# Layer 1 of the last chunk as a Strassen product, interleaved with layer 2 of the chunk ahead of it

## The chip, the cores and the metric

The kernel runs on one core of one Trainium2 chip. A core has five engines that matter here, each with its own in-order list of instructions: TensorE (PE, matmuls; its weight loads are shown apart as PEld), VectorE (DVE), ScalarE (ACT), GpSimd (POOL) and SyncE (SP, which here only starts DMAs). They meet through semaphores. TensorE writes to PSUM, eight banks of 512 fp32 columns; the other data are in SBUF. The metric is the device time of one execution in microseconds (us).

## The reference

The kernel computes attention and then a two-layer perceptron on its output.

- Attention: q, k, v are [8 batches, 8 heads, 576 tokens, 64]. Heads 0 to 3 see the last 32 positions, heads 4 to 7 see every 32nd earlier position; softmax, then the product with v.
- The heads are put side by side: x is [4608 tokens, 512].
- Layer 1: h = x @ w_in with w_in [512, 2048], then g = max(h, 0) + alpha * min(h, 0), with one alpha for each of the 2048 columns.
- Layer 2: out = g @ w_out with w_out [2048, 512], fp32.

## The kernel before, in words

Everything is written out by hand: each instruction goes through `keep`, which holds the program's order, so each engine executes its instructions in the order in which the Python code emits them. There is no scheduler that moves them.

The 4608 tokens are nine chunks of 512 (`NCH`, n = 0 to 8). Attention writes x transposed into a ring `xT`. For each chunk the main loop has 30 steps i. In steps 0 to 15 `lin1_piece` (L694 and after) makes one piece m of layer 1: 128 of the 2048 columns for 512 tokens, by four matmuls of 512 columns (`lin1_mm`, L678) into one of three PSUM banks `hb` that are used in turn. ScalarE then makes neg = Relu(-h) into one of three buffers in turn (L697), and VectorE makes g = neg * (1 - alpha) + h as fp16 into `gT` (L700). That last operation is not emitted at once: it is put in a list `late` and emitted a little later, when the next attention step or the end of the step empties the list.

In steps 16 to 29 `lin2_sums` makes layer 2 of the same chunk as a Strassen product in Winograd's form (for chunks 1 to 8). Tokens and the 2048 inner columns are cut in halves, and so is the output: seven products p0 to p6 stand for the eight quarter products. Each product has two row blocks (mt) of eight matmuls of 256 columns (L811), one row block for each step. The products need sums of quarters of g (`g_sum`, L760; the array `gsum`, called g1 to g4 here) and of quarters of w_out, which are made once. Three banks A, B and C collect the products: A takes p0, then p2, p4 and p6 on top of it, and between them it is copied out or added (L823 on ScalarE after p0, p1, p2 and p6; L826 on VectorE after p3, p4, p5). A bank may be written again only when the reader before has finished. Most of g1 is made by GpSimd during layer 1 (steps 5, 9 and 13); the rest of g1 and g2, g4, g3 are made by VectorE, emitted in the first steps of layer 2.

Between these steps `attn_n` emits pieces of attention for later batches. They run out during layer 2 of chunk 6: the last masks of the scores (L470, L477) are GpSimd's last work there. Chunks 7 and 8 have no attention beside them.

In chunk 8, layer 2 uses a further bank (`opl`) so that its results go out by halves.

Of the kernel before, what the change touches and what calls it, by code (L numbers as in the profile page):

```python
# [9 lines left out]
F32 = mybir.dt.float32  # L10
F16 = mybir.dt.float16
ALU = mybir.AluOpType
AF = mybir.ActivationFunctionType
# [19 lines left out]
def kernel(  # L33
# [36 lines left out]
    id16 = cpool.tile([16, 16], F32)  # L70
    alpha_r = cpool.tile([16, 128], F32)
    oma = cpool.tile([128, 16], F32)
    mmul = cpool.tile([128, 360], F16)
    madd = consts[:, 128:488]
    ident = consts[:, 0:128]
# [18 lines left out]
    NE = 6  # L94
# [2 lines left out]
    LX = 5  # L97
    qTs = [cpool.tile([128, 2, 672], F16, name=f"qT{i}") for i in range(2)]
    kTs = [cpool.tile([128, 2, (768, 672)[i]], F16, name=f"kT{i}") for i in range(2)]
    vls = [cpool.tile([128, 24, 65], F16, name=f"vl{i}") for i in range(2)]  # L100
    vss = [cpool.tile([128, 4, 8, 65], F16, name=f"vs{i}") for i in range(2)]
    ets = [cpool.tile([128, 800], F16, name=f"et{i}") for i in range(NE)]
    x16s = cpool.tile([80, 1024], F16)
    qks = {nm: cpool.tile([80, 4, 512], F16, name=f"{nm}sd") for nm in "qk"}

# [318 lines left out]
    late = []  # L424
# [152 lines left out]
    for g in range(7, npair + 2):  # L577
        c = g // 4
        a, p, t = g, g - 1, g + 1
# [69 lines left out]
    def attn_until(b):  # L649

        return max(i for i, (g, _) in enumerate(pieces) if g == 4 * b + 3) + 1

    def attn_step(end):
        run_masks()
        if pos["i"] < end:
            pieces[pos["i"]][1]()
            pos["i"] += 1
        while late:
            late.pop(0)()
        if defer:  # L660
            defer.pop(0)()


    gTs = {}
# [23 lines left out]
    def lin1_piece(n, m):  # L688
        if n not in gTs:
            gTs[n] = gpool.tile([128, 16, 512], F16, tag="gT", name="gT")  # L690
        if n == 0 and m < 3:
            hps = lin1_mm(n, m, (0,), False, True)
        else:
            hps = lin1_mm(n, m, (2, 3, 0, 1) if n == 1 else range(4), True, True)  # L694

        neg = npool.tile([128, 512], F32, tag="neg", name="neg")
        keep(nc.scalar.activation(neg, hps, AF.Relu, scale=-1.0))  # L697

        def fin():
            keep(nc.vector.scalar_tensor_tensor(  # L700
                gTs[n][:, m, :], neg, oma[:, m : m + 1], hps, op0=ALU.mult, op1=ALU.add))
        late.append(fin)
# [33 lines left out]
    def w_sums(eng, which):  # L736

        w1, w2, w4 = wsum
        w3 = wq(0, 1)
        steps = {  # L740
            1: (w1, wq(0, 1), wq(0, 0), ALU.subtract),
            2: (w2, wq(1, 1), w1, ALU.subtract),
            3: (w3, wq(1, 1), wq(0, 1), ALU.subtract),
            4: (w4, wq(1, 0), w2, ALU.subtract),
        }
        for z in which:
            o, x, y, op = steps[z]
            keep(eng.tensor_tensor(o, x, y, op=op))
# [26 lines left out]
    def lin2_sums(n, i):  # L775
# [69 lines left out]
        else:  # L845
# [7 lines left out]
            elif mt:  # L853
                store(n, 1, 0, o21)

    def load_w(c, second, half=None):
# [23 lines left out]
    def load_unit(b, strided, v_too=True):  # L880
# [3 lines left out]
        if v_too:  # L884
# [7 lines left out]
            name=nc.get_next_instruction_name(), act_func_set_id=6, ins=[], outs=[]  # L892
# [120 lines left out]
    load_unit(3, False, False)  # L1013


    for n in range(1, NCH):
        ab = attn_until(n + 1) if n + 1 < B else len(pieces)
        left = ab - pos["i"]
        acc = 0.0
        if n == 1:  # L1020
            w_sums(nc.vector, (3,))
        for i in range(30):
            second["on"] = i >= 16
            if i < 16:
                lin1_piece(n, {13: 7, 14: 14}.get(i, 8 * (i % 2) + i // 2))
                if i in (5, 9, 13) and (n, i) != (1, 13):
                    g_sum(nc.gpsimd, n, 1, i // 2 - 2, i // 2)
                if n == 1 and i == 14:
                    load_v(3, False)
            else:  # L1030
                lin2_sums(n, i - 16)
                if n == 1 and i == 20:
                    load_v(3, True)
            if n < B - 2 or i < 16 or i > 19:
                if n != 1 or i not in (16, 17):
                    acc += left / ((22.5 if i < 16 else 16.9) if n == 1 else 16 if n == B - 2 else 20.5) * (
                        0.5 if i < 16 else 1.0)
            cnt = int(acc)
            acc -= cnt
            attn_n(cnt, ab)  # L1040
        while pos["i"] < ab:
            attn_step(ab)


# [28 lines left out]
```

The softmax here doesn't subtract the row's maximum and nothing guards it: scores larger than these inputs give would overflow.

## Time and profile before

The median of three executions is 298.58 us (297.83 to 298.62). The profiled execution has a span of 296.6 us.

| Stretch of the span, us | what TensorE does | VectorE busy, us | ScalarE busy, us | GpSimd busy, us |
|---|---|---|---|---|
| 227.6 to 241.0 | layer 2 of chunk 6, the last of attention | 10.88 | 3.94 | 1.44 |
| 241.0 to 254.8 | layer 1 of chunk 7 | 10.58 | 9.64 | 3.47 |
| 254.8 to 267.0 | layer 2 of chunk 7 | 7.43 | 2.36 | 0 |
| 267.0 to 280.8 | layer 1 of chunk 8 | 10.54 | 9.54 | 3.47 |
| 280.8 to 296.6 | layer 2 of chunk 8, last outputs | 8.06 | 3.05 | 0 |

In the first four stretches TensorE is busy from end to end; in the last it is busy for 12.34 of 15.80 us, the rest being the last copy and the last DMA. The granted clock of TensorE is 1.00 in the first four.

A row of a group of instructions reads: line, engine, operation, what it writes <- what it reads, shape, count | busy time in us, mean ns of one | idle time of the engine ahead of it, and what ended that. In a row of the order of time the first number is the start in us from the start of the span, the second the length of the row.

### The profile page before, as it was taken

What the parts mean: (1) busy time and instruction counts of PE and PEld (TensorE: products, weight loads), DVE (VectorE), ACT (ScalarE), POOL (GpSimd) and SP (SyncE); (2) the same over time, 40 slices, a digit from 0 to 9 for tenths busy, and PEclk for the clock granted to TensorE, in tenths of its full rate; (3) what the DMA queues carried; (4) which work ended last, traced back from release to release, by engine and by line L of the source; (5) the groups of instructions that cost most, each with busy time, mean ns of one, the idle gap of its engine ahead of it and who ended that gap; (6) DMA issues with size and microseconds to landing.
All of it is one profiled execution on the core that took longest, in us unless ns stands there. A gap on an engine that the chain in (4) does not pass through costs nothing.

```text
span 296.6 us, 7099 instructions
## 1 busy us (share of the span) xinstructions
PE 289.7 (98%) x2808; PEld 193.9 (65%) x2808; DVE 227.8 (77%) x427; ACT 173.7 (59%) x325; POOL 168.0 (57%) x174
## 2 busy tenths in 40 slices
PE   7899999999999999999999999999999999999995
PEld 3564456645885487647898887468746864784584
DVE  6788869979966987588848884889488858936872
ACT  3566558889557763775367637763676157406620
POOL 8972269379738996688767777765564003101300
PEclk9999999999999999999999999999999999999999
DMA  7999999996998989999999999993811140022004
GB/s 217 208 200 207 205 239 262 180 198 233 119 139 146 167 89 159 175 151 165 147 222 146 147 132 194 202 127 64 192 22 21 25 141 0 2 74 71 0 2 141
DMA packets 102529, 41.01 MB, mean 138 GB/s; under 512 B 80720, under 2 KB 99424, under 8 KB 102496
## 3 DMA queue, kind: packets, MB, share of 16 engines
q0 software_dynamic: 56048, 18.20, 60.3%
q1 hardware_dynamic: 46176, 21.83, 38.1%
q10 hardware_dynamic: 272, 0.52, 0.6%
q8 instruction: 22, 0.36, 0.6%
q14 instruction: 11, 0.09, 0.1%
HBM read 38.60 MB, written 9.44 MB: 162 GB/s over the span
## 4 chain that ended last, share of the span: by engine, by line
PE 89%; DVE 4%; DMA 2%; ACT 2%; issue 1%; SPq 0%; ACTq 0%
PE hb L678 38%; PE hb L811 30%; PE hb L715 5%; PE pv L512 4%; DMA kl<-in_k_dram 2%; PE sp L450 2%; PE hx L678 2%; PE tp L280 2%; PE xp L533 1%; DVE gT L700 1%; PE opl L811 1%; PE sph L450 1%; DVE gsum L760 1%; PE pv L508 1%; ACT neg L697 1%
## 5 line engine op out<-in xcount | busy, mean ns | idle before, releaser
L678 PE MATMUL hb<-xT,win 128*128 128x512 f16 (+1 forms) x616 | 127.2, 357 | 0.0
L700 DVE SCALAR_TENSOR_TENSOR gT<-neg,oma,hb 128x512 f16<-128x512 f32 x138 | 100.6, 744 | 33.0 <-ACT neg L697 26.3
L697 ACT ACTIVATE neg<-hb 128x512 f32<-128x512 f32 x138 | 82.1, 598 | 32.7 <-PE hb L678 31.5
L678 PEld LDWEIGHTS <-win 128*128 128x128 f16 x640 | 59.9, 98 | 53.8
L760 POOL TENSOR_TENSOR gsum<-gT 128x512 f16<-128x512 f16 x23 | 26.5, 1150 | 68.8 <-DVE gT L700 68.8
L811 PEld LDWEIGHTS <-gsum 128*128 128x128 f16 x512 | 47.5, 98 | 5.9 <-DVE gsum L760 0.2
L811 PEld LDWEIGHTS <-gT 128*128 128x128 f16 x384 | 35.9, 98 | 6.0 <-issue 0.5
L470 POOL TENSOR_TENSOR et<-et,mmul 128x576 f16<-128x576 f16 (+1 forms) x24 | 30.5, 1273 | 12.9 <-issue 6.5
L823 ACT COPY o<-hb 128x512 f32<-128x512 f32 (+1 forms) x32 | 18.1, 569 | 32.5 <-PE hb L811 32.5
L523 DVE TENSOR_TENSOR x<-pv,rc 96x384 f16<-96x384 f32 (+2 forms) x65 | 34.5, 531 | 2.2
L811 PE MATMUL hb<-wout,gT 128*128 128x256 f16 x248 | 30.8, 273 | 0.1
L811 PE MATMUL hb<-wout,gsum 128*128 128x256 f16 x248 | 30.5, 272 | 0.2 <-ACT o L823 0.2
L811 PE MATMUL hb<-wsum,gsum 128*128 128x256 f16 x248 | 30.1, 273 | 0.0
L477 POOL TENSOR_TENSOR et<-et,mmul 72x576 f16<-72x576 f16 (+2 forms) x24 | 29.4, 1227 | 0.4 <-ACT et L474 0.4
L826 DVE TENSOR_TENSOR o<-hb,o 128x512 f32<-128x512 f32 (+1 forms) x24 | 16.3, 680 | 17.0 <-PE hb L811 12.5
L464 ACT ACTIVATE et<-sp 72x576 f16<-72x576 f32 (+2 forms) x24 | 16.4, 685 | 20.6 <-PE sph L450 17.2
L512 PEld LDWEIGHTS <-et 72*128 72x128 f16 (+1 forms) x416 | 21.8, 98 | 8.1 <-issue 1.3
L474 ACT ACTIVATE et<-sph 72x288 f16<-72x288 f32 (+2 forms) x48 | 17.8, 388 | 0.0
L521 DVE RECIPROCAL rc<-pv 72x6 f32<-72x6 f32 (+2 forms) x80 | 14.5, 181 | 2.7 <-PE pv L512 2.4
L715 PE MATMUL hb<-wout,gT 128*128 128x512 f16 x64 | 15.6, 379 | 0.3 <-ACT osb L720 0.3
L811 PE MATMUL hb<-wsum,gT 128*128 128x256 f16 x120 | 15.3, 273 | 0.0
L217 POOL COPY vs<-stv 72x1024 f16<-72x1024 f16 x12 | 12.1, 1031 | 4.0 <-DMA stv<-in_v_dram 4.0
(116 smaller groups left out, 320.2 us busy)
## 6 DMA issues: line engine op xcount, KB each, us to landing
out_dram<-o SPq DMA_DIRECT2D x31, 256.0 KB, 3.4
stv<-in_v_dram POOLq DMA_DIRECT2D x8, 288.0 KB, 8.4
vl<-in_v_dram POOLq DMA_DIRECT2D x6, 384.0 KB, 9.2
kl<-in_k_dram SPq DMA_DIRECT2D x4, 512.0 KB, 5.4
wout<-in_moe_w_out_dram POOLq DMA_DIRECT2D x4, 512.0 KB, 16.2
qsd<-in_q_dram POOLq DMA_DIRECT2D x6, 288.0 KB, 7.7
ksd<-in_k_dram POOLq DMA_DIRECT2D x6, 288.0 KB, 8.1
win<-in_moe_w_in_dram POOLq DMA_DIRECT2D x3, 512.0 KB, 12.2
```

The costliest lines, as they stand in the source:

```text
L470: keep(nc.gpsimd.tensor_tensor(mv, mv, m, op=ALU.mult))
L474: keep(nc.scalar.activation(ev[:, n * y : n * y + n], sps[y][0:r, 0:n], AF.Exp, scale=SCALE))
L477: keep(nc.gpsimd.tensor_tensor(mv, mv, m, op=ALU.mult))
L512: keep(nc.tensor.matmul(pv[:, 65 * x : 65 * x + 65], et[0:r, c : c + 128], v16[0:r, 2 * P.pr + hh, t, :] if P.strided else v16[:, 6 * (2 * ...
L523: keep(nc.vector.tensor_tensor(P.x16[0:w, c0 : c0 + 64 * nb].rearrange("r (c e) -> r c e", e=64), pvv[:, :, 0:64], rc[0:w, 0:nb].unsqueeze ...
L678: keep(nc.tensor.matmul(hps[:, dst : dst + w], win16[:, kk, 128 * m : 128 * m + 128], xT[:, kk, src : src + w], start=(first and kk == kks ...
L697: keep(nc.scalar.activation(neg, hps, AF.Relu, scale=-1.0))
L700: keep(nc.vector.scalar_tensor_tensor(gTs[n][:, m, :], neg, oma[:, m : m + 1], hps, op0=ALU.mult, op1=ALU.add))
L715: keep(nc.tensor.matmul(ops, gTs[n][:, kf, 128 * mt : 128 * mt + 128], wout16[:, kf, :], start=(kf == 0), stop=(kf == 15)))
L760: keep(eng.tensor_tensor(o[:, k0:k1], x[:, k0:k1], y[:, k0:k1], op=op))
L811: keep(nc.tensor.matmul(dst, lhs[:, kf, 128 * mt : 128 * mt + 128], rhs[:, kf, :], start=(first and own and kf == 0), stop=(kf == 7), skip ...
L823: keep(nc.scalar.copy(o, x))
```

## The change

Layer 1 of chunk 8 (called `NL`) is made by the same kind of product. The 512 input columns, the 512 tokens and the 2048 output columns are cut in halves; the output columns are further cut into four units v = 0 to 3, so that one unit has 256 columns of each half. A unit has seven products p0 to p6 of four matmuls of 256 columns each (`lin1_sums`). It needs four sums of quarters of w_in (`unit_sum`, on GpSimd) and, shared by all units, four sums of quarters of x (`x_sum`, on VectorE).

These products are no longer a stretch of their own: each step of layer 2 of chunk 7 is followed by two of them, so 14 steps hold all 28. Their results are collected in bank A (two banks in turn, for even and odd units), B and C. ScalarE copies A, B, A out after p0, p1 and p2; VectorE adds B, A, C onto these copies after p3, p4 and p5; p6 is finished from the bank itself. The activation then follows for each finished quarter [128, 2 x 256]: ScalarE's Relu and two half-width operations on VectorE, or, for p3 of every unit and p5 of units 1 and 3, four operations on GpSimd (twice min and times -(1 - alpha), with the scalar `noma`, then a sum). These last operations are deferred by `late` to just ahead of the next product.

The new g, `gT2`, would need SBUF of its own while chunk 7's is still in use; it takes the place of the attention buffers `vls`, `vss` and the sixth `ets`, which become views of it. The sums take buffers that attention used in the pools for q, k, x and v.

```diff
+    gT2 = cpool.tile([128, 16, 512], F16, name="gT2")
+    gflat = gT2.rearrange("p k c -> p (k c)")
+    vls = [gflat[:, 1560 * i : 1560 * i + 1560].rearrange("p (b e) -> p b e", e=65) for i in range(2)]
...
+    ets = [cpool.tile([128, 800], F16, name=f"et{i}") for i in range(NE - 1)] + [gflat[:, 7280:8080]]
...
+        bank, lhs, rhs, first = (
+            ("A", wh(v, 0, 0), xh(0, 0), True),
+            ("B", g1, xsums[0], True),
+            ("A", g2, xsums[1], False),
+            ("B", g4, xh(1, 1), False),
+            ("A", g3, xsums[2], False),
+            ("C", wh(v, 0, 1), xh(1, 0), True),
+            ("A", wh(v, 1, 1), xsums[3], False),
+        )[p]
+        t = hid[bank][v % 2]
+        for mm in range(2):
+            for kk in range(2):
+                keep(nc.tensor.matmul(
+                    t[:, 256 * mm : 256 * mm + 256], lhs[:, kk, 128 * mm : 128 * mm + 128], rhs[:, kk, :],
+                    start=(first and mm == 0 and kk == 0), stop=(kk == 1), skip_group_check=True))
+        tv = t.rearrange("p (m c) -> p m c", m=2)
+        if p < 3:
+            keep(nc.scalar.copy(hid[("o11", "o22", "o12")[p]], tv))
+            return
+        i, l = ((0, 1), (1, 1), (0, 0), (1, 0))[p - 3]
+        if p < 6:
+            o = hid[("o12", "o22", "o11")[p - 3]]
+            keep(nc.vector.tensor_tensor(o, o, tv, op=ALU.add))
+        else:
+            o = tv
+        neg = npool.tile([128, 2, 256], F32, tag="neg", name="neg")
+        pool = p == 3 or (p == 5 and v % 2 == 1)
+        if not pool:
+            keep(nc.scalar.activation(neg, o, AF.Relu, scale=-1.0))
+
+        def fin(o=o):
+            for mm in range(2):
+                m = 8 * i + 2 * v + mm
+                g = gT2[:, m, 256 * l : 256 * l + 256]
+                if pool:
+                    keep(nc.gpsimd.tensor_scalar(
+                        neg[:, mm], o[:, mm], 0.0, noma[:, m : m + 1], op0=ALU.min, op1=ALU.mult))
+                    keep(nc.gpsimd.tensor_tensor(g, neg[:, mm], o[:, mm], op=ALU.add))
+                else:
+                    keep(nc.vector.scalar_tensor_tensor(
+                        g, neg[:, mm], oma[:, m : m + 1], o[:, mm], op0=ALU.mult, op1=ALU.add))
+
+        late.append(fin)
...
+            if n == NL and i < 16:
+                continue
...
+            if n == NL - 2 and i >= 26:
+                unit_sum(nc.gpsimd, 0, i - 26)
+            if n == NL - 1:
+                if i < 16 and i % 2:
+                    unit_sum(nc.gpsimd, 1 + i // 8, i % 8 // 2)
+                if i == 4:
+                    keep(nc.vector.tensor_scalar(noma, oma, -1.0, None, op0=ALU.mult))
+                if i in (6, 8, 10, 12):
+                    x_sum(nc.vector, i // 2 - 3)
+                if 20 <= i < 24:
+                    unit_sum(nc.gpsimd, 3, i - 20)
+                if i >= 16:
+                    for v, p in slots[2 * (i - 16) : 2 * (i - 16) + 2]:
+                        while late:
+                            late.pop(0)()
+                        lin1_sums(v, p)
+                        if p == 1 and 0 < v:
+                            g_sum(nc.gpsimd, NL, 1, 2 * v - 2, 2 * v)
```

More of the change, by code (lines that the diff above doesn't have):

```diff
@@ L72 @@
     oma = cpool.tile([128, 16], F32)
+    noma = cpool.tile([128, 16], F32)
     mmul = cpool.tile([128, 360], F16)
@@ L99 @@
     kTs = [cpool.tile([128, 2, (768, 672)[i]], F16, name=f"kT{i}") for i in range(2)]
-    vls = [cpool.tile([128, 24, 65], F16, name=f"vl{i}") for i in range(2)]
-    vss = [cpool.tile([128, 4, 8, 65], F16, name=f"vs{i}") for i in range(2)]
-    ets = [cpool.tile([128, 800], F16, name=f"et{i}") for i in range(NE)]
+    gT2 = cpool.tile([128, 16, 512], F16, name="gT2")
+    gflat = gT2.rearrange("p k c -> p (k c)")
+    vls = [gflat[:, 1560 * i : 1560 * i + 1560].rearrange("p (b e) -> p b e", e=65) for i in range(2)]
+    vss = [gflat[:, 3120 + 2080 * i : 5200 + 2080 * i].rearrange("p (h t e) -> p h t e", h=4, t=8)
+           for i in range(2)]
+    ets = [cpool.tile([128, 800], F16, name=f"et{i}") for i in range(NE - 1)] + [gflat[:, 7280:8080]]
     x16s = cpool.tile([80, 1024], F16)
@@ L854, in lin2_sums, with wh, xh, unit_sum @@
                 store(n, 1, 0, o21)
+    NL = NCH - 1
+    units, xsums, hid = {}, [], {}
+    def wh(v, i, j):
+        return win16[:, 2 * j : 2 * j + 2, 1024 * i + 256 * v : 1024 * i + 256 * v + 256]
+    def xh(j, i):
+        c0 = (512 * NL) % RING + 256 * i
+        return xT[:, 2 * j : 2 * j + 2, c0 : c0 + 256]
+    def unit_sum(eng, v, z):
+        if v not in units:
+            units[v] = hpool.tile([128, 4, 2, 256], F16, tag=("ql", "kl")[v % 2], bufs=2, name="us")
+        g1, g2, g3, g4 = [units[v][:, k] for k in range(4)]
+        o, x, y, op = (
+            (g1, wh(v, 1, 0), wh(v, 1, 1), ALU.add),
+            (g2, g1, wh(v, 0, 0), ALU.subtract),
+            (g3, wh(v, 0, 0), wh(v, 1, 0), ALU.subtract),
+            (g4, wh(v, 0, 1), g2, ALU.subtract),
+        )[z]
+        keep(eng.tensor_tensor(o, x, y, op=op))
@@ new lines, in x_sum, with lin1_sums @@
+    def x_sum(eng, z):
+        xsums.append(tpool.tile([128, 2, 256], F16, tag="tl", name="xsum"))
+        o, x, y = (
+            lambda: (xsums[0], xh(0, 1), xh(0, 0)),
+            lambda: (xsums[1], xh(1, 1), xsums[0]),
+            lambda: (xsums[2], xh(1, 1), xh(0, 1)),
+            lambda: (xsums[3], xh(1, 0), xsums[1]),
+        )[z]()
+        keep(eng.tensor_tensor(o, x, y, op=ALU.subtract))
+    def lin1_sums(v, p):
+        if not hid:
+            sp = pbpool.tile([128, 2, 512], F32, tag="sp", name="spl")
+            hid["A"] = [sp[:, y] for y in range(2)]
+            for nm in "BC":
+                hid[nm] = [pspool.tile([128, 512], F32, tag="ps", name="hid")] * 2
+            gTs[NL] = gT2
+        if p == 0:
+            for nm in ("o11", "o22", "o12"):
+                if v % 2 == 0:
+                    hid[nm] = xpool.tile([128, 2, 256], F32, tag="x16", name=nm)
+                elif nm != "o12":
+                    big = spool.tile([128, 2, 2, 256], F32, tag="v", bufs=2, name=nm)
+                    hid[nm], hid["o12"] = big[:, 0], big[:, 1]
+        g1, g2, g3, g4 = [units[v][:, k] for k in range(4)]
+        bank, lhs, rhs, first = (
[39 more added lines that the diff above has]
+        late.append(fin)
@@ L1013 @@
     load_unit(3, False, False)
+    slots = [(v, p) for v in range(4) for p in range(7)]
     for n in range(1, NCH):
@@ L1042 @@
             attn_step(ab)
+        while n == NL - 1 and late:
+            late.pop(0)()
 _INS = ['q', 'k', 'v', 'moe_w_in', 'moe_w_out', 'moe_alpha']
```

## The prediction

> **What bounds the kernel now.** I read the page first, then the chain that ended last, cut to the last 100 us. Its columns are start, duration and engine, tile and line.
>
> ```profile
> PE 289.7 (98%) x2808; PEld 193.9 (65%) x2808; DVE 227.8 (77%) x427; ACT 173.7 (59%) x325; POOL 168.0 (57%) x174
> ```
> ```profile
> 227.68 5.32 PE hb L811 x48
> ...
> 241.06 13.81 PE hb L678 x64
> 254.87 12.23 PE hb L811 x112
> 267.10 13.81 PE hb L678 x64
> 280.91 0.87 PE hb L811 x8
> ```
>
> TensorE is the bound, with no hole from chunk 7 to the end. Layer 1 (L678) is 64 matmuls of 512 columns in 13.81 us; layer 2 (L811), already a Strassen product, 112 of 256 columns in 12.23 us, 0.109 us each. So any stall of TensorE from here on is paid in full, and what matters is whether the other engines keep up in the new order. Their durations come from the groups of instructions between 241.0 and 254.8 us (layer 1 of chunk 7) and between 254.8 and 267.0 us (its layer 2); a row ends with the busy time and the mean ns of one, and after the bar the idle time before them:
>
> ```profile
> L700 DVE SCALAR_TENSOR_TENSOR gT<-neg,oma,hb 128x512 f16<-128x512 f32 x15 | 11.2, 747 | 4.4 <-ACT neg L697 2.9
> L697 ACT ACTIVATE neg<-hb 128x512 f32<-128x512 f32 x15 | 9.0, 597 | 4.0 <-PE hb L678 4.0
> L760 POOL TENSOR_TENSOR gsum<-gT 128x512 f16<-128x512 f16 x3 | 3.5, 1155 | 21.6 <-DVE gT L700 21.6
> ```
> ```profile
> L826 DVE TENSOR_TENSOR o<-hb,o 128x512 f32<-128x512 f32 x3 | 2.1, 691 | 3.7 <-PE hb L811 2.1 <-issue 1.6
> L823 ACT COPY o<-hb 128x512 f32<-128x512 f32 x3 | 1.8, 586 | 3.5 <-PE hb L811 3.5
> ```
>
> Last, what VectorE and GpSimd do to each other, from two stretches of the order of time (around 107 us, then around 143 us):
>
> ```profile
> 107.34 0.52 DVE L760 TENSOR_TENSOR gsum<-gT 128x512 f16<-128x512 f16 x1
> 107.53 1.46 POOL L477 TENSOR_TENSOR et<-et,mmul 72x576 f16<-72x576 f16 x1
> 107.78 2.36 DVE L760 TENSOR_TENSOR gsum<-gsum,gT 128x1024 f16<-128x1024 f16 x2
> ```
> ```profile
> 142.91 1.21 DVE L760 TENSOR_TENSOR gsum<-gT 128x2048 f16<-128x2048 f16 x1
> ...
> 143.00 1.54 POOL L468 TENSOR_TENSOR et<-et,mmul 128x192 f16<-128x192 f16 x1 [1.93 <-ACT et L464]
> ```
>
> The pair of sums at 107.78 takes 1.28 us elsewhere and 2.36 here: it waited for the GpSimd product that ends at 108.99. The small product at 143.00 takes 0.55 us elsewhere and 1.54 here: it waited for the sum that ends at 144.12.
>
> **What the Trainium skill says.** "SBUF — State Buffer", Who interferes with whom: a VectorE instruction with two SBUF inputs and a GpSimd instruction that reads SBUF exclude each other for the whole instruction. The two cases above agree. "PSUM — Partial Sum Buffer", Engine vs sequencer instructions: the queues of ScalarE, VectorE and GpSimd are strict FIFO, so what waits at a head holds all behind it. "GPSIMD Engine Reference", Elementwise — side-by-side cycle accounting: a two-input operation there is limited by the one read port, 4497 ns for 2048 columns; 1155 ns for 512 here agrees. Its table under Engine selection calls one-input operations roughly line rate.
>
> **Part by part.** *Removed*: 64 matmuls, 13.81 us. *Added*: 4 units x 7 products x 4 = 112 matmuls of 256 columns, 112 x 0.1092 = 12.23. **-1.6 us**, if nothing waits.
>
> *Buffers shared with attention.* In the built order, instructions and waits before chunk 6 are the same but for one wait on GpSimd, for work done long before. Nothing.
>
> *Sums of W_in, 16 on GpSimd, 1.15 us each.* They wait for no data, so the first four start when GpSimd is free, not with the step that names them: after the last mask, at 229.05 us. There they meet VectorE's five g_sums of chunk 6 (229.52 to 233.53), which TensorE takes the moment they end: g1 ends at 229.93 and its matmul starts at 229.99. Taken in turns, as at 107 us: sum 1 holds until 230.15, g1 ends 230.45 (matmul wanted it at 230.1: 0.4 lost), sum 2 to 231.5, first half of g2 232.05 (0.45 more), sum 3, second half 233.65 (1.15), sum 4, g4 235.8 (0.7). **2.7 us**; if VectorE kept its turn after g1, 0.4. I take 2.7.
>
> *Sums of x, 4 on VectorE in layer 1 of chunk 7.* One takes 0.43 us by L760's row of that size. A piece is 0.863 us, VectorE's own work 0.67 of it, and a bank is wanted again 0.25 us after it is freed (L700 ends at 243.40, the fourth piece begins at 243.65). Alone they lose about 0.2 in all. But GpSimd is nearly full here (8 sums of W_in, 3 of g) and two of the four find it in the middle of one: about 0.6 and 0.8. **1.4 us**, ends 0.2 and 2.0.
>
> *The interleaved stretch*: 14 steps of 8 matmuls of layer 2 and two products of 4, 1.747 us each. Banks: A takes p0, p2, p4, p6, and each waits for the reading of the one before. I follow the queues from its start (0), 0.1 us per hand-over. Half-width L700 is worked out as 0.48 us (0.747 less half the slope of L826: 0.69 for 512, 0.425 for 256 columns); a GpSimd half-width sum 0.66 (half of 0.97, and 0.18 fixed).
> - VectorE first has the last two L700, then g1, g2, g2, g4 until 4.4, the add of p3 to 5.0, g3 to 6.15; only then the add of p4, 6.1 to 6.76. p6 wanted to start at 6.1. **0.7**.
> - Unit 0 to unit 1. In order: add p4 6.76, Relu 7.4, two L700 halves 8.3, add p5 8.9 (queued behind them), its Relu 9.6, layer 2's copy 10.1, Relu p6 10.7, then the copies of unit 1's p0, 11.3. ScalarE can't reach that copy earlier, though p0 was done at 7.7. TensorE's p2 wanted it at 9.0: 2.3 lost. The halves read neg and the output from SBUF, so they take turns with GpSimd's four operations for p3 and its sums: 3.2. **2.7**, the middle.
> - Unit 1 to 2: p5 is on GpSimd, the chain is short: **0.3**.
> - Unit 2 to 3: as above without layer 2's copy and the g_sums: 4.8 us from the end of p4 to the copy, 3.5 are there: 1.4. With GpSimd behind: from step 4 to step 8 it has four sums of W_in, two of g and unit 1's two products, 6 x 1.15 + 2 x 2.2 = 11.3 us in 8.7, so it reaches unit 2's p3 some 3 us late; Relu p6 needs the neg buffer that p3 held (three in turn, the fourth use comes back to the first): 3.2. **2.3**.
> - The end. Unit 3's p5 goes over GpSimd, and the first product of the last layer 2 needs its blocks 6 and 7. From the end of p4: add 0.8, Relu 1.4, halves 2.35, add p5 2.95, then GpSimd 2 x (0.45 + 0.62) = 2.1: 5.1, wanted at 2.5: 2.6. With p3's operations and contention ahead of it 3.6. **3.1**. Before, this edge had no hole (280.91 follows 267.10 + 13.81).
>
> *Not in the trace*: the pointer tensor_scalar (min, times) on GpSimd. Its nearest rows are L217's copy of 1024 columns in 1.03 us (0.39 for 256, with the 0.18 fixed) and the one tensor_scalar, L968, 1.44 for 360 (1.07 for 256). I take 0.45, near the low end, because the skill's "line rate" points there; at 1.07 each of the six products that GpSimd finishes takes 1.2 us more, which by the same queues is 2 us at the end and 3 to 4 before unit 3.
>
> Sum: -1.6 + 2.7 + 1.4 + 0.7 + 2.7 + 0.3 + 2.3 + 3.1 = **+11.6**, 298.6 to about **310**.
>
> **Rivals.** (1) Only the queues' order costs, GpSimd and VectorE hardly hinder each other: -1.6 + 0.4 + 0.2 + 0.7 + 2.3 + 1.4 + 2.7 = +6.1, 304.7. For it: of the g_sums in the trace most met no GpSimd; against it: there GpSimd was idle then, and here it has some 22 us of work in 24.5. (2) GpSimd's tensor_scalar is slow: 310 + 5 to 7 = 316. For it L968; against it, that was its first call, of another operation, in f16. (3) TensorE doesn't wait: buffers and slack suffice, 298.6 - 1.6 = 297.0, with some of the small waits 297.5. For it: the mean load of VectorE (some 22 of 24.5 us) and of ScalarE (15) leaves room. Against it: the waits are latencies in in-order queues, not loads, and 3.5 us between p4 and the next unit's p2 don't hold a chain of 4.8.
>
> **How the numbers follow.** Forecast 0.57, rival 1 0.22, rival 2 0.12, rival 3 0.09. The forecast spans 306 to 314 by its ends. 303.5 to 316 takes it, rival 1 and the lower edge of rival 2, and leaves out rival 3 and most of 2, about 0.19. Rival 3 gives faster 0.08 and no change 0.01; the others slower, 0.91.
>
> **What would show it.** TensorE's matmuls of layer 1 at 0.109 us each; holes on TensorE at about 230 to 235 us (ended by VectorE's g_sums), in layer 1 of chunk 7 (by L700), and in the interleaved stretch before p2 of units 1 and 3 (ended by ScalarE's copy, which stands behind a Relu that waits for VectorE), and one at the first product of the last layer 2, ended by GpSimd. Single g_sums above 1.5 us show the exclusion. I am wrong if the interleaved stretch takes under 26 us, or if GpSimd's output operations for a product take well under 2 us and TensorE finds the copies done.

## The result, and the profile after

The changed kernel takes 331.67 us (median of four executions, 330.81 to 332.88), against 298.3 us for the kernel before: a ratio of 1.1123, 95% interval 1.1083 to 1.1163. The forecast was about 310 us, with a range from 303.5 to 316; the direction was right and the size was not.

These rows of the changed kernel's page answer to those shown of before: the engines' loads, the granted clock of TensorE in 40 slices of the span (tenths of full speed), and the two groups that have the most idle time ahead of them in the new part.

```profile
PE 298.1 (90%) x2856; PEld 201.7 (61%) x2856; DVE 242.7 (74%) x448; ACT 176.7 (54%) x331; POOL 213.5 (65%) x214
...
PEclk9999999999999999999999999999999976896789
...
L947 POOL TENSOR_SCALAR neg<-o,noma 128x256 f32<-128x256 f32 x12 | 15.9, 1328 | 19.0 <-DVE o L934 19.0
...
L924 PE MATMUL spl<-xT,win 128*128 128x256 f16 x16 | 3.7, 379 | 14.7 <-DVE gT L951 14.7
```

TensorE is no longer busy from end to end: 90% against 98%, although it has less to do. Two things stand here that the kernel before did not have. The clock falls in the last fifth of the span (from about 264 us). And the first product of a unit (L924, `spl<-xT,win`, which is p0) waits 14.7 us in all for L951, VectorE's last output operation of a unit.

Where the 33.1 us of span came from, by TensorE's own stages:

| Stage | before, us | after, us | difference |
|---|---|---|---|
| layer 2 of chunk 6 | 13.38 | 16.46 | +3.08 |
| layer 1 of chunk 7 | 13.81 | 15.09 | +1.28 |
| layer 2 of chunk 7 with layer 1 of chunk 8 | 26.04 | 46.78 | +20.74 |
| last layer 2 to the end | 15.85 | 23.9 | +8.05 |

The third stage is the bulk. These are TensorE's holes there and at the end, in order of time (in brackets the idle time ahead, and what ended it); lines without a hole are left out:

```profile
265.90 0.60 PE L924 MATMUL spl<-xsum,win 128*128 128x256 f16 x4 [0.61 <-DVE o L934]
272.69 1.04 PE L924 MATMUL spl<-xT,win 128*128 128x256 f16 x4 [6.19 <-DVE gT L951]
...
285.66 1.04 PE L924 MATMUL spl<-xT,win 128*128 128x256 f16 x4 [3.46 <-DVE gT L951]
...
298.03 1.04 PE L924 MATMUL spl<-xT,win 128*128 128x256 f16 x4 [5.06 <-DVE gT L951]
...
310.73 0.40 PE L815 MATMUL hb<-wout,gT 128*128 128x256 f16 x1 [4.11 <-POOL gT L949]
313.34 0.39 PE L815 MATMUL hb<-wout,gT 128*128 128x256 f16 x1 [2.21 <-POOL gT L949]
```

The first hole is p6 of unit 0, as forecast. The next three are ahead of p0 of units 1, 2 and 3, not ahead of p2, and what ends them is not ScalarE's copy but the last operation of the unit before. Read the lengths too: four products of 256 columns take 0.60 us at 265.90 and 1.04 us at 272.69, 285.66 and 298.03. After each hole of this size TensorE runs at half speed for a while. From 257 us on about 70 products of 256 columns are followed by the next one after 0.21 us instead of 0.109; together they cost 7.2 us.

The summary by stretch of time shows the same (length, then busy time and count of PE, PEld, DVE, ACT, POOL, then clock):

```profile
257.50:313.30 55.80, 34.19 (x239) 26.19 (x237) 30.79 (x46) 16.70 (x29) 35.72 (x34) 0.78 0.06 19
```

In 55.8 us no engine is busy for more than 36. Nothing is full; the engines wait for each other.

### The profile page after: what moved, and what is told of

Read it like the earlier page. It is cut to its first block, busy times and chain, and to the rows that moved or that the text cites. A ratio compares the mean times of both kernels' runs of the same rounds, so it can differ in the third digit from the quotient of the medians.

```text
span 329.7 us, 7284 instructions
## 1 busy us (share of the span) xinstructions
PE 298.1 (90%) x2856; PEld 201.7 (61%) x2856; DVE 242.7 (74%) x448; ACT 176.7 (54%) x331; POOL 213.5 (65%) x214
## 5 line engine op out<-in xcount | busy, mean ns | idle before, releaser
L682 PE MATMUL hb<-xT,win 128*128 128x512 f16 (+1 forms) x552 | 113.5, 354 | 0.9 <-DVE gT L704 0.9
L704 DVE SCALAR_TENSOR_TENSOR gT<-neg,oma,hb 128x512 f16<-128x512 f32 x122 | 88.5, 743 | 28.1 <-ACT neg L701 23.9
L701 ACT ACTIVATE neg<-hb 128x512 f32<-128x512 f32 x122 | 72.6, 598 | 29.8 <-PE hb L682 28.3
L682 PEld LDWEIGHTS <-win 128*128 128x128 f16 x576 | 53.6, 98 | 47.8 <-issue 1.5
L527 DVE TENSOR_TENSOR x<-pv,rc 96x384 f16<-96x384 f32 (+2 forms) x65 | 34.5, 531 | 2.2
L815 PE MATMUL hb<-wsum,gsum 128*128 128x256 f16 x248 | 33.1, 284 | 1.7 <-DVE gsum L764 1.7
L815 PE MATMUL hb<-wout,gsum 128*128 128x256 f16 x248 | 31.6, 276 | 0.4 <-DVE gsum L764 0.4
L947 POOL TENSOR_SCALAR neg<-o,noma 128x256 f32<-128x256 f32 x12 | 15.9, 1328 | 19.0 <-DVE o L934 19.0
L516 PE MATMUL pv<-gT,et 72*128 72x65 f16 (+1 forms) x350 | 21.5, 194 | 0.2
L481 POOL TENSOR_TENSOR et<-et,mmul 72x576 f16<-72x576 f16 (+2 forms) x16 | 18.8, 1177 | 0.0
L924 PE MATMUL spl<-xT,win 128*128 128x256 f16 x16 | 3.7, 379 | 14.7 <-DVE gT L951 14.7
L764 DVE TENSOR_TENSOR gsum<-gT 128x512 f16<-128x512 f16 (+2 forms) x17 | 16.4, 965 | 0.2
```

What stands on the lines that cost most here:

```text
L481: keep(nc.gpsimd.tensor_tensor(mv, mv, m, op=ALU.mult))
L516: keep(nc.tensor.matmul(pv[:, 65 * x : 65 * x + 65], et[0:r, c : c + 128], v16[0:r, 2 * P.pr + hh, t, :] if P.strided else v16[:, 6 * (2 * ...
L527: keep(nc.vector.tensor_tensor(P.x16[0:w, c0 : c0 + 64 * nb].rearrange("r (c e) -> r c e", e=64), pvv[:, :, 0:64], rc[0:w, 0:nb].unsqueeze ...
L682: keep(nc.tensor.matmul(hps[:, dst : dst + w], win16[:, kk, 128 * m : 128 * m + 128], xT[:, kk, src : src + w], start=(first and kk == kks ...
L704: keep(nc.vector.scalar_tensor_tensor(gTs[n][:, m, :], neg, oma[:, m : m + 1], hps, op0=ALU.mult, op1=ALU.add))
L764: keep(eng.tensor_tensor(o[:, k0:k1], x[:, k0:k1], y[:, k0:k1], op=op))
```

## The experiments

Fifteen kernels, in four groups. A ratio is against the kernel before, with its 95% interval.

### Which part costs what

**The shared buffers alone.** `gT2` and its views stay; chunk 8 is computed as before, without new sums or products.

```diff
+        if n == NCH - 1:
+            gTs[n] = gT2
-            if n == NL and i < 16:
-                continue
...
-            if n == NL - 2 and i >= 26:
-                unit_sum(nc.gpsimd, 0, i - 26)
...
```

> The kernel before with attention's buffers as views of gT2 and chunk 8's g written there, all else as before: no sums of w_in or x, layer 1 of chunk 8 plain. If the shared buffers cost nothing, as the prediction had it: 298.3 us, within 0.3%. If they bring waits between attention and the views: above 300, with holes on TensorE before 227 us.

Measured: 298.35 us, 1.0012 [0.9985, 1.0038]. No cost of the buffers shows.

**The sums alone.** As above, but the sums of w_in and of x are made too. Nobody uses them, and layer 1 of chunk 8 is the plain one.

> As the kernel with the views alone, and the sixteen sums of w_in on GpSimd, the four of x on VectorE and noma as in the change, with nobody reading them; layer 1 of chunk 8 plain. If the two earlier stages' losses come from these sums (they took 3.1 us more in layer 2 of chunk 6 and 1.3 in layer 1 of chunk 7): 302.7 us. The last four sums of w_in then lie in layer 2 of chunk 7 beside its g sums and may add up to 1. If the earlier losses only shift waits that would come later anyway: 298 to 300.

Measured: 306.47 us, 1.0261 [1.0223, 1.03]: 8.1 us over the kernel with the buffers alone, for work that TensorE has no part in, and 3.8 over the 302.7 of the expectation. The losses in layer 2 of chunk 6 and in layer 1 of chunk 7 are those of the changed kernel. Where at most 1 us was expected, the last four sums of w_in meet VectorE's sums of chunk 7 in the same way as the first four do those of chunk 6: layer 2 of chunk 7 takes 15.25 us instead of 12.23. What happens is seen best in the changed kernel; here are VectorE's and then GpSimd's order of time in layer 2 of chunk 6:

```profile
229.48 0.92 DVE L764 TENSOR_TENSOR gsum<-gT 128x512 f16<-128x512 f16 x1
230.32 3.19 DVE L764 TENSOR_TENSOR gsum<-gsum,gT 128x1024 f16<-128x1024 f16 x2
233.55 2.06 DVE L764 TENSOR_TENSOR gsum<-gT,gsum 128x2048 f16<-128x2048 f16 x1
```
```profile
230.19 1.22 POOL L883 TENSOR_TENSOR us<-us,win 128x512 f16<-128x512 f16 x1
231.37 1.60 POOL L883 TENSOR_TENSOR us<-win 128x512 f16<-128x512 f16 x1
232.93 1.60 POOL L883 TENSOR_TENSOR us<-win,us 128x512 f16<-128x512 f16 x1
```

The pair at 230.32 takes 1.28 us when GpSimd is idle and 3.19 here, and GpSimd's sums grow from 1.15 to 1.60: each waits for the other in turn. TensorE then waits for `gsum`, 0.41, 0.29, 0.95 and 0.42 us.

**The sums moved out of each other's way, all else as in the changed kernel.**

```diff
-            if n == NL - 2 and i >= 26:
-                unit_sum(nc.gpsimd, 0, i - 26)
+            if n == NL - 2 and i in (0, 20):
+                if i:
+                    keep(nc.gpsimd.tensor_copy(scr[:, 0:1], gsum[3][:, 7, 255:256]))
+                for z in range(3, 9) if i else range(3):
+                    unit_sum(nc.gpsimd, z // 4, z % 4)
```

(In chunk 7 the x sums come first, at step 0, and the rest of the w_in sums before step 12. The small copy reads the last of the g sums, so that GpSimd starts only when VectorE has done them.)

> The changed kernel itself with nothing else altered than where the sums of W_in and of x stand: ahead of the g sums that they met. Theory: the losses in layer 2 of chunk 6 (3.1 us) and in layer 1 of chunk 7 (1.3) go, all else stays: 331.7 - 4.4 = 327.3, or down to 325 if the four sums that stood in the interleaved stretch held it up too. Rival (the sums' wait only hides another one there, the last weights or the g sums themselves): 330 or more.

Measured: 326.44 us, 1.0941 [1.0887, 1.0995], 5.2 us less. (There are two executions, 324.73 and 328.15 us, so the size is known to some 1.6 us only.) In the trace the two stages are as before the change, and p0 of unit 1 waits 5.42 us instead of 6.19. The sums are a true cost, but about a sixth of the whole.

### The wait ahead of p0

Both banks of A, for even and odd units, are slices of one tile of two banks. The changed kernel's p0 of unit 1 starts at 272.69 us, as soon as VectorE has read p6 of unit 0, which lies in the other bank:

```profile
271.77 0.86 DVE L951 SCALAR_TENSOR_TENSOR gT<-neg,oma,spl 128x256 f16<-128x256 f32 x2
```

The built program has the same wait: p0 of unit 1 writes the second half of the tile and waits for the readers of p6 of unit 0 in the first half. If that is a wait for the tile and not for the data, another tile must remove it.

```diff
-            hid["A"] = [sp[:, y] for y in range(2)]
+            hid["A"] = [sp[:, 0], pspool.tile([128, 512], F32, tag="ps", name="hia")]
```

> The changed kernel with bank A of units 1 and 3 in a PSUM tile of its own instead of the second half of the two-bank tile. If each unit's first product waits for the whole unit before it because both halves count as one tile: the holes of 6.2, 3.5 and 5.1 us before p0 vanish, and what is left of them stands before p2, behind the ScalarE queue, about 7 us in all; some 320 us. If the prediction's chain (ScalarE's copy behind a Relu) was what really held TensorE: the holes only move from p0 to p2 and the time stays at 329 to 332.

Measured: 321.49 us, 1.0766 [1.0716, 1.0817], 10.2 us less. TensorE's holes are now:

```profile
265.58 0.60 PE L924 MATMUL spl<-xsum,win 128*128 128x256 f16 x4 [0.60 <-DVE o L934]
270.47 0.60 PE L924 MATMUL hia<-xsum,us 128*128 128x256 f16 x4 [2.55 <-ACT o L929]
278.46 0.60 PE L924 MATMUL spl<-xsum,us 128*128 128x256 f16 x4 [1.28 <-ACT o L929]
290.02 1.01 PE L924 MATMUL hia<-xsum,us 128*128 128x256 f16 x4 [5.67 <-ACT o L929]
300.54 0.28 PE L815 MATMUL hb<-wout,gT 128*128 128x256 f16 x1 [2.98 <-POOL gT L949]
303.16 0.40 PE L815 MATMUL hb<-wout,gT 128*128 128x256 f16 x1 [2.33 <-POOL gT L949]
```

No wait ahead of p0 is left. The one that the prediction described, p2 waiting for ScalarE's copy (L929), is there now. It had been hidden behind a longer one. Its sizes are 2.55, 1.28 and 5.67 us, where 2.7, 0.3 and 2.3 were forecast. The last is long because the Relu of p6 waits for a neg buffer that GpSimd still reads; ScalarE's order of time there:

```profile
288.90 0.60 ACT L940 ACTIVATE neg<-spl 128x512 f32<-128x512 f32 x1 [2.62 <-POOL gT L949]
289.39 0.58 ACT L929 COPY o<-hia 128x512 f32<-128x512 f32 x1
```

### GpSimd's operations, and the clock

**No output on GpSimd.** All quarters go over ScalarE's Relu and VectorE.

```diff
-        pool = p == 3 or (p == 5 and v % 2 == 1)
+        pool = False
```

> The changed kernel with no output on GpSimd: ScalarE's Relu and two VectorE operations for p3 and p5 as well. If GpSimd's slow tensor_scalar (1.3 us each) makes the hole at the first product of the last layer 2 (6.3 us): that hole falls to about 2.5 us, the holes between the units stay at 4 to 6 each since VectorE and ScalarE do the work in a longer chain, and the whole is 325 to 328 us. If GpSimd's share is also what makes the holes between units, these fall below 3 us each and the whole to 315 to 320.

Measured: 333.04 us, 1.1153 [1.1076, 1.123]: the expectation failed, it is not faster at all. The hole before the last layer 2 shrinks, but p6 of every unit now waits for VectorE (1.0 to 3.1 us), with twelve half-width operations more on VectorE, and p0 still waits for the whole unit (5.4, 3.2 and 4.1 us). Moving the outputs from GpSimd to VectorE doesn't remove the holes between units. The run doesn't show what a shorter GpSimd operation alone would save.

**Other forms of GpSimd's first operation.** For p3 of each unit the min-and-multiply is replaced, so the activation of these quarters differs from the reference; the point is only the duration.

```diff
+                            neg[:, mm], o[:, mm], 0.0, -0.85, op0=ALU.min, op1=ALU.mult))
...
+                            neg[:, mm], o[:, mm], noma[:, m : m + 1], None, op0=ALU.mult))
...
+                            neg[:, mm], o[:, mm], 0.0, None, op0=ALU.min))
...
+                        keep(nc.gpsimd.tensor_copy(neg[:, mm], o[:, mm]))
```

> The changed kernel with GpSimd's first operation for p3 changed by unit, to time its forms: unit 0 min and multiply by an immediate, unit 1 one multiply by the pointer, unit 2 one min with an immediate, unit 3 a copy; p5 as before. The activation of these quarters is left out or changed. If the second operation or the pointer makes it slow: 1.15 us for two operations, about 0.45 for one and for the copy (256 columns, 1 ns each and 0.18 fixed). If every tensor_scalar on GpSimd is slow: 0.9 to 1.2 in all but the copy.

Measured: 328.72 us in a single execution, which is too few for a verdict. GpSimd's order of time, the second of each pair:

```profile
267.87 1.24 POOL L948 TENSOR_SCALAR neg<-o 128x256 f32<-128x256 f32 x1
...
281.18 1.08 POOL L951 TENSOR_SCALAR neg<-o,noma 128x256 f32<-128x256 f32 x1
...
286.13 1.14 POOL L959 TENSOR_SCALAR neg<-o,noma 128x256 f32<-128x256 f32 x1
...
291.91 0.85 POOL L954 TENSOR_SCALAR neg<-o 128x256 f32<-128x256 f32 x1
...
303.47 0.40 POOL L957 COPY neg<-o 128x256 f32<-128x256 f32 x1
```

L948 is min and mult with constants, L951 one mult by a pointer (a scalar read from a tile), L959 the original (here of p5), L954 one min, L957 the copy. Only the copy takes 0.40 us; the simplest tensor_scalar of the same 256 columns takes twice that. "GPSIMD Engine Reference", Engine selection, in the Trainium skill, calls one-input operations roughly line rate; for the copy that may stand, for tensor_scalar this run shows otherwise. The run also bears on the end: with the copies in p3 of unit 3 the two holes there are 3.69 and 1.54 us instead of 4.11 and 2.21, while p0 still waits 6.03, 3.06 and 4.85 us.

**Fill the holes with products that nobody needs.** 18, 8 and 14 products of 512 columns ahead of p0 of units 1, 2 and 3, and 10 in the first hole at the end, into a bank that is never read. All waits stay.

```diff
+        if p == 0 and v:
+            fill((18, 8, 14)[v - 1])
...
+            if last and i == 0 and kf == 6:
+                fill(10)
```

> The changed kernel with 50 extra matmuls of 512 columns into an unused bank: 18, 8 and 14 just ahead of p0 of units 1, 2 and 3 (3.9, 1.7 and 3.0 us, inside the holes there), 10 inside the hole at the first product of the last layer 2. The output is unchanged. If TensorE's clock falls because it idles: no hole is longer than 2.9 us any more, the matmuls after each hole take 0.109 us instead of 0.212, and the time falls by about 7 us to some 324, although work was added. If the lower clock comes from anything else: 331 to 333, matmuls after the holes still at 0.212.

Measured: 327.37 us, 1.0977 [1.0948, 1.1006]: 4.3 us faster with 50 products more. TensorE's order of time at unit 1, and after the end's holes:

```profile
266.40 4.05 PE L905 MATMUL fill<-win 128*128 128x512 f16 x18
272.77 0.61 PE L938 MATMUL spl<-xT,win 128*128 128x256 f16 x4 [2.32 <-DVE gT L965]
...
304.72 0.28 PE L817 MATMUL hb<-wout,gT 128*128 128x256 f16 x1 [1.96 <-POOL gT L963]
307.33 0.40 PE L817 MATMUL hb<-wout,gT 128*128 128x256 f16 x1 [2.33 <-POOL gT L963]
309.23 4.62 PE L817 MATMUL hb<-wsum,gsum 128*128 128x256 f16 x24
```

p0 still starts at 272.8, but now at full speed (0.61 us). At the end, where two holes of 2 us with hardly a product between them were left, the clock still fell: 24 products took 4.62 us, at full speed 2.78. In all 25 products ran at half speed there and cost 2.6 us, most of what is missing to 324. "TensorE: Matmul & The Clock Gate", Part 1, in the skill says that the clock goes to half after an idle window of some 3.4 us whose phase is free. The traces agree in the main, with shorter holes than that: every hole of 3.14 us or more in these runs was followed by half speed, and none of up to 3.06 us that stood alone. But 2.2 to 2.3 us were enough where a hole of 0.7 to 1.3 stood some 3 us ahead (the kernel without outputs on GpSimd, and the first rearrangement below), or one of 2 us as here. These three cases fit a rule by the share of idle time better than one by a single unbroken stretch; no run tests that by itself.

### Can the saving come out as time?

The change makes 112 products of 256 columns where 64 of 512 stood, as much as 16 of 256 fewer, which should give 1.6 us once nothing waits. The first of these kernels starts from the one with two tiles, and each of the others from the one ahead of it, but for one that is marked; most changes are of order. All compute the whole reference again.

**Two tiles, cheaper outputs, other order.** No tensor_scalar on GpSimd: ScalarE makes Relu with the scale -(1 - alpha), so that GpSimd or VectorE only adds, or VectorE makes max(h, alpha * h) in one operation (right for slopes up to 1; here they are 0 to 0.3). ScalarE's parts of p5 and p6 stand behind the copies of the next unit.

```diff
+                keep(nc.vector.scalar_tensor_tensor(
+                    g, o[:, mm], alph[:, m : m + 1], o[:, mm], op0=ALU.mult, op1=ALU.max))
...
+                keep(nc.scalar.activation(neg[:, mm], o[:, mm], AF.Relu, scale=noma[:, m : m + 1]))
...
+            if p == 1 and "5" in pend:
+            if p == 2 and "6" in pend:
```

> On top of the kernel with two tiles for bank A: the same activation without GpSimd's tensor_scalar and without ScalarE standing behind VectorE. p4 and p5 of units 2, 3 are one pass of VectorE for each half (larger of h and alpha h); p3 and p5 of units 0, 1 are ScalarE's Relu with the scale -(1-alpha) and one sum on GpSimd; p6 likewise with VectorE's sum; and the ScalarE parts of p5 and p6 are emitted after the next unit's copies. Sums of w_in and x stay where they are. If in-order queues and the slow GpSimd operation are all that was left: holes only from the sums (4.4 us in the two earlier stages), 0.6 at p6 of unit 0 and 1 to 1.5 at the end; about 304 us. If VectorE's and GpSimd's exclusion in the interleaved stretch is a bound of its own: above 307.

Measured: 307.16 us, 1.0302 [1.0279, 1.0325], 24.5 us under the changed kernel and 14.3 under the one with two tiles. How much of the 14.3 is order and how much the cheaper outputs, no run separates. The expectation of some 304 was missed, and 307.16 is just in the range that was to show exclusion as a bound of its own; the last kernel below argues against that. Left are the sums' losses, 0.6 and 0.7 at p6, and 2.3 at the end with 1.7 of half speed after it.

**With the sums out of the way** (most of their new places as shown above) and layer 2's sums of chunk 7 later:

> On top of that: the sums of w_in and x moved out of each other's way (six sums of w_in behind a one-element copy that waits for chunk 6's last g sum, the four x sums in VectorE's idle time at the start of layer 1 of chunk 7, the next sums of w_in behind them, three in the interleaved stretch), g4 and g3 of chunk 7 emitted three and four steps later, and unit by unit three steps, so that the products end one step before layer 2 does. If the causes found are all of it, what is left is the saving of 16 matmuls: 296.5 us (296 to 297.5), 0.3 to 0.7% under the kernel before. If exclusion and hand-overs remain: 298 to 301.

Measured: 300.62 us, 1.0077 [1.006, 1.0094], where 296.5 was expected. Everything up to the interleaved stretch takes as long as before the change. Left in it: 1.58 us for the late sum g3, 0.76 at p6, 0.83 at the end.

**All sums before the stretch.**

```diff
-            if n == NL - 2 and i == 20:
+            if n == NL - 2 and i in (0, 20):
...
-                if i in (20, 21, 22):
```

> The kernel of e8_best with three sums of W_in moved into layer 1 of chunk 6 and the last three ahead of the interleaved stretch, and the layer-2 sums of chunk 7 one step earlier. Theory (what was left in e8_best was VectorE held off by GpSimd's sums in the stretch): the 1.58 us hole before the second layer of chunk 7 shrinks below 0.4, the end keeps about 1 us, and the time is 297.0 (296.5 to 298). Rival (GpSimd's outputs and their exclusion with VectorE hold it whatever the sums do): 299 to 301.

Measured: 300.2 us, 1.0062 [1.0043, 1.0082]: hardly anything, and not the 297.0 of the theory. The 1.58 us hole is gone and smaller ones stand elsewhere, in the time that the rival had.

**p5 on VectorE.**

```diff
-            if v < 2:
+            if v < 0:
```

> As e9_sums_early, but product p5's outputs go to VectorE in every unit, so that GpSimd does no output of it. If exclusion between GpSimd and VectorE is what stretches VectorE's operations, VectorE's own pairs fall back to about 0.9 us and the time is at or below e9_sums_early's (297). If it is VectorE's load, the holes between units grow and it is 299 or more.

Measured: 301.08 us, 1.0086 [1.0066, 1.0105]. VectorE's half-width operations get a little shorter, in the mean 703 ns against 798, but there are 16 of them for 12. The intervals of the two kernels overlap; exclusion and load can't be told apart by this pair.

**p5 early.** This one starts from the kernel with all sums before the stretch, with p5's output on GpSimd in every unit. p5 needs no sum and adds only to p0's copy. It goes to the second place of a unit, so that the quarter that the last layer 2 reads first is there long before.

```diff
-        for z, ps in enumerate(((0, 1), (2, 3), (4, 5), (6,))):
+        for z, ps in enumerate(((0, 5), (1, 2), (3, 4), (6,))):
```

> The kernel of e9_sums_early with the products of a unit in the order 0, 5, 1, 2, 3, 4, 6 (p5 needs no sum and adds only to p0's output, so the quarter that the last layer 2 reads first is there before the unit ends), with p5's outputs on GpSimd in every unit, the layer-2 sums of chunk 7 at steps 1 and 2 where VectorE was idle, and VectorE's output additions of chunk 7 behind those of the unit in the same step. In e9_sums_early five holes of 3.37 us in all are left, and its time less these is 296.8, 1.4 under the kernel before. Theory (VectorE's order, not its total load, makes these holes): the 1.5 us before the last layer 2 go, and half of the rest: 297.5 (296.6 to 298.5). Rival (VectorE, stretched by GpSimd, is simply full in the stretch): the holes move, and it is 300 again.

Measured: 299.92 us, 1.0048 [1.0032, 1.0064], where 297.5 was expected. The hole at the end is gone; p4 now waits for ScalarE's copy of p2, which stood behind the Relu of p5, in every unit.

**The copy of p2 before that Relu**, and g3 one step later.

```diff
-            if p == 1 and "5" in pend:
+            if p == 2 and "5" in pend:
```

> The kernel of e12_p5_early with two orders changed: ScalarE copies p2's sum before it does the Relu of p5 (p4 waited for that copy in every unit, 0.25 to 0.6 us each), and the sum g3 of chunk 7 goes one step later on VectorE, behind the addition that p6 of unit 0 waited for. Nothing is removed: VectorE's, ScalarE's and GpSimd's load is the same. If queue order makes the last 2.9 us of holes, they go but for about 0.5 and the time is 297.4 (296.6 to 298.0): the 16 products saved then show as time, about 1.1 us under the kernel before. If load is what is left, the holes move and it stays at 299.5 to 300.

Measured: 298.47 us, 0.9998 [0.998, 1.0015]: equal to the kernel before, and still above the expected 296.6 to 298.0. Four holes of 0.3 us (from start to start) are left, at p6.

**p6 behind p0 and p5 of the next unit.**

```diff
-    for u in range(4):
+    for u in (3, 2, 1, 0):
...
+            slots.setdefault(3 * u + z + (u == 3 and z == 3), []).extend((u, p) for p in ps)
```

> The kernel of e13_copy_first with p6 of each unit behind p0 and p5 of the next unit (0.9 us later), so that VectorE's addition of p4, for which p6 waited some 0.3 us in every unit, is done. No work is changed. If TensorE's stretch is then free of waits, 1.2 of the 1.6 us of saved matrix work that the holes still take come out: 297.4 (296.8 to 298.1), ratio 0.996. If the load is the limit, the wait moves to the next sum and it stays at 298.5.

Measured: 299.22 us, 1.002 [1.0, 1.0039]: the expectation failed. p6 waits no more, but its bank comes free later and p0 two units on waits for it:

```profile
268.05 0.60 PE L934 MATMUL spl<-xT,win 128*128 128x256 f16 x4 [0.72 <-DVE gT L959]
274.62 0.60 PE L934 MATMUL hia<-xT,win 128*128 128x256 f16 x4 [0.73 <-DVE gT L959]
```

**The Relu of p6 at once, and VectorE's addition for it first.** ScalarE was idle when p6 ended.

```diff
-            def later(o=o):
-                neg = scaled(6, o)
-                return lambda: larger(nc.vector, 6, neg, o)
-            pend["6"] = later
+            neg = scaled(6, o)
+            pend["m"] = lambda: larger(nc.vector, 6, neg, o)
...
-            if p == 2 and "6" in pend:
+            if p == 2 and "m" in pend:
```

> The kernel of e14_p6_later, whose two holes of 0.9 us stood before p0 of units 2 and 3 (VectorE's addition for p6 two units back stood behind two others), with ScalarE's Relu of p6 issued as soon as p6 is, VectorE's addition for it ahead of those of p3 and p4, and the last output addition of chunk 7 not deferred. Only the order changes. If order is the limit, 2.0 us of holes go: 297.3 (296.7 to 298.0), ratio 0.996, and the saving of the 16 products is real. If the holes move once more and it stays at 298.4 to 299.3, the change can't be made to pay by reordering alone.

Measured: 297.12 us against 298.71, 0.995 [0.9932, 0.9969]: faster than the kernel before by 1.6 us. The page, and the summary of the interleaved stretch:

```profile
PE 287.9 (98%) x2856; PEld 198.8 (67%) x2856; DVE 232.6 (79%) x441; ACT 180.7 (61%) x345; POOL 196.6 (67%) x200
...
PEclk9999999999999999999999999999999999999999
```
```profile
254.30:279.00 24.70, 24.70 (x228) 22.14 (x227) 22.33 (x33) 18.48 (x39) 14.30 (x11) 1.00 0.10 33
```

TensorE is busy from end to end again, with the same 2856 products as in the changed kernel, and VectorE, at 22.3 of 24.7 us, keeps up. The stretch takes 24.46 us (254.30 to 278.76) where it took 26.04: 1.58 us less, as the count of products has it.

## Why the prediction was wrong, point by point

*The buffers, nothing*: right (the first experiment).

*Removed and added, -1.6 us "if nothing waits"*: right, and shown by the last kernel, whose interleaved stretch has no hole.

*The sums of W_in, 2.7, and of x, 1.4*: right in mechanism and size, 3.08 and 1.28. "Taken in turns" held nearly operation by operation: at the four sums TensorE lost 0.58, 0.45, 1.11 and 0.59 us from start to start, where 0.4, 0.45, 1.15 and 0.7 were forecast. The rule that the prediction took from the skill's "SBUF — State Buffer", Who interferes with whom, agrees with these numbers.

*p6 of unit 0, 0.7*: right, 0.61.

*Unit 0 to 1, 1 to 2, 2 to 3*: this is the step that failed. The prediction asked when ScalarE could reach the copy of p0, found "TensorE's p2 wanted it at 9.0: 2.3 lost", and took 2.7, 0.3 and 2.3 us. It followed A as two banks, each with its own readers. In the program they are one tile, and p0 of a unit waits for the last reading of the unit before in the other bank. So TensorE doesn't begin a unit before VectorE has finished with p6 of the one before: 6.19, 3.46 and 5.06 us, 14.7 where 5.3 were forecast. The order of the instructions with their waits would have shown it. The kernel with two tiles settles it: the holes ahead of p0 go, and the forecast chain appears in their place, ended by the instruction that it named, with 2.55 us for the 2.7 forecast at unit 1. There the sizes for the later units were too small (1.28 and 5.67). The Relu ahead of each of these copies waited for GpSimd, 2.86 and 2.62 us; the term that comes next is the likely reason, though no run changes it alone there.

*GpSimd's tensor_scalar, 0.45 us "near the low end"*: mis-sized. It took 1.33 in the mean. One row of the trace pointed there (L968, 1.07 when scaled to 256 columns), the other was a copy, and the runs show that a copy takes much less, 0.40. (The addition after it, put at 0.66 in one place and 0.62 in another, took 0.72.) It is the main term behind *the end*, 3.1 forecast and 6.3 measured: for p3 and p5 GpSimd works for 8.6 us without a break, from 304.71 to 313.28, and TensorE waits for the last of it. With copies in place of p3's operations these holes came to 5.2. But this is not what makes most of the loss: with no output on GpSimd at all the time stayed at 333.04, though there VectorE had the work instead.

*Not in the prediction at all*: the clock. The holes between units and the pair at the end cost more than themselves, 7.2 us in all. The filled holes show that idleness is the cause: p0 started at the same time at unit 1, but ran at full speed.

The sum of these for the changed kernel: -1.6 + 4.4 for the sums + 15.3 of holes in the stretch + 6.3 at the end + 7.2 of clock = 31.6 of the 33.1 us of span. Of the other 1.5, about 1.1 is the tail of the last product ahead of each hole, which the trace counts as busy: from start to start the holes are 0.16 to 0.29 us longer than their idle time. Some 0.4 stays open. Against the forecast, the waits between units were 9.4 us too small, the clock 7.2 and the end 3.2.

Of the rivals, the first, in which GpSimd and VectorE hardly hinder each other, is answered by the 3.08 and 1.28 us. The second, a slow tensor_scalar, was right on the duration, and 316 was still too little since it shared the forecast's view of the banks and left out the clock. The third, no wait, had against it that "the waits are latencies in in-order queues, not loads". That was right for this order, and it also says why the last kernel could remove them though VectorE's load, 22.3 of 24.7 us, is the 22 of 24.5 that the prediction named.

## What to carry to other kernels

When a part of a kernel alternates between two buffers, look whether they are two tiles or two slices of one: in this kernel slices of one waited for each other as if they were one buffer, and the waits of the built program showed this before any run. Price a hole of TensorE of over about 3 us, by the changed kernel's trace, at its own length plus 1.1 to 2.7 us for the half speed after it. And where all engines have slack but the time grows, as here (36 of 56 us at most), look at the order of the queues first, one wait at a time, until the wait that is named by the trace is gone. Here two tiles, cheaper outputs and new orders together took 34.5 us off a change whose gain was 1.6.

## What the runs showed that I had not expected

- Half speed after a hole lasted 2.4 to 5.6 us in the changed kernel, 11 to 26 products of 256 columns at a spacing of 0.212 us instead of 0.109. Two holes of 2 us each, with one product between them, were followed by 25 such products in the kernel with filled holes, more than the 19 after the hole of 5.06.
- GpSimd on 256 fp32 columns: copy 0.40 us, tensor_scalar with one constant 0.85, one pointer 0.94 to 1.08, two operations mostly 1.14 to 1.31 (up to 2.05 beside VectorE's sums), tensor_tensor mostly 0.72. An addition of two tensors is cheaper than the simplest tensor_scalar.
- VectorE's pair of half-width scalar_tensor_tensor takes 0.88 us alone and 1.9 to 2.1 beside GpSimd additions, in two of the four units of the last kernel and in all four of the two with p5 early and with the copy of p2 first. In the last kernel it did no harm, since TensorE's stretch has no hole.
- An order can be wrong in both directions: p6 one place later removed its wait of 0.3 us and made one of 0.7 us two units on, in the same bank.
